# A convolution, SoLU and layer-norm kernel: separate scales for the first chunk's two pieces, another order of its loads, and the gain moved into the mean's matrix

## The chip, the cores and the metric

The kernel runs on one core of a Trainium2 chip. The metric is the time of one execution on the device in microseconds (us), and lower is better. The engines are TensorE (PE, with its weight loads PEld), VectorE (DVE), ScalarE (ACT) and GpSimd (POOL); SyncE (SP) issues the transfers.

## The reference

```
w   = softmax over the 7 taps of weight (8 heads x 7 taps)
y   = causal 7-tap convolution of x (8 x 4160 x 192); 24 channels share a head's taps
h   = y.reshape(33280, 192) @ w_in                    # 192 x 1024
s   = h * softmax(h)                                  # per token, over 1024
ln  = (s - mean(s)) / sqrt(var(s) + 1e-6) * g_ln
out = ln @ w_out                                      # 1024 x 192
```

All inputs and the output are float32.

## The kernel before

**Precision.** Each float32 matrix is split into two float16 parts, an upper and a lower one, and a product is three passes (upper by upper, upper by lower, lower by upper). A power of two scales each matrix first: x of a chunk by `s`, w_in by `t_in`, w_out by `t_out`. A scale comes from a sum of squares: an activation with an accumulator, a matmul with `ones` that adds over partitions (`total`, L95), one reduction, and four operations of one column on DVE (`root_power`, L105 to L112). `cv` holds five numbers of a chunk that follow from `s` and `t_in`, the exponent's factor among them. The inputs' words are taken apart by integer operations (class `Words`: exponents L447, mantissas L452, signs L480, join L489, value L496, powers L486, low words L458).

**Tiles.** The 33280 tokens are 260 tiles of 128. A tile goes through: twelve matmuls into its pair of PSUM banks `ph` (L736, L759; L749 for tiles 0 and 1), max over 1024 columns (DVE L790), exponential with its sum (ACT L797), product with its sum (DVE L807), cast to float16 (ACT L815), sum of squares (ACT L819), lower part (POOL L827), a transposing transfer to `pT` (L829), the matmuls of the second product `po` (L843), and its evacuation to SBUF (DVE L850), where two partial sums of 192 columns are added. Rows are finished by a group (L898, L902, L917, L921) and stored. I write max(3) for L790 of tile 3, mul(3) for its L807.

**Order.** Each engine's program is the order in which the code is written. Tiles 0 to 7, chunk 0 of x (1024 tokens, in two pieces of five windows of 112), have start-up code of their own: `first_two`, `second_two`, `third_two` and `fourth_two`. Then a loop takes three tiles a step, and `last_three` ends it. There are three pairs of PSUM banks (0 to 2) and two single banks. `emit_first` fills pairs for tiles 0 and 1, `emit_two` for the next two, and `hold` puts two groups of chunk 1's convolution (L281) into a pair. A pair is free again when its tile's mul has read it.

**Start-up.** SP issues the loads: x's first piece, w_in in two halves (512 KB each, `raw_in`), its last 64 rows (two of 256 KB), x's second piece (480 KB) between them, and w_out (`raw_out`, 1536 KB). DVE takes apart w_in's words, makes chunk 0's `s` and then `t_in`, writes the lower parts of the convolved x (L322; upper ones L313 on ACT) and of w_in (L647). POOL forms `cv` (L208) and w_out's values (`whole` L474, `value` L496, behind a `gate` that waits for the signs). `out_mean` (L701) multiplies w_out by `even`, whose every entry is 1/1024, so that each column's mean is in every partition; `out_upper` (L710) subtracts it. Before this, `out_powers` (L685) multiplies w_out's powers by g_ln.

Of the kernel before, what the change touches and what calls it, by code (L numbers as in the profile page):

```python
# [8 lines left out]
F16 = mybir.dt.float16  # L9
# [10 lines left out]
def kernel(  # L20
# [9 lines left out]
    nc = tc.nc  # L30
# [92 lines left out]
    class Chunk:  # L123
# [14 lines left out]

        def load(self, j):
# [52 lines left out]
        def scale_steps(self):  # L192
# [3 lines left out]
            ch = self.ch  # L196
            one = lambda nm, tag: sp.tile([P, 1], F32, name=f"{nm}_{ch}", tag=tag, bufs=2)
            self.all, self.s = one("xm", "xm"), one("s", "s")
            self.cv = cv = sp.tile([P, 5], F32, name=f"cv_{ch}", tag="cv", bufs=4)
# [3 lines left out]
                lambda: dve.tensor_reduce(self.all, self.tp, AX.X, ALU.add),  # L203
                *root_power(self.s, self.all, 2.0**30, 1e-14),
                lambda: dve.tensor_scalar(cv[:, 2:3], self.s, t_in, None, ALU.mult),
# [13 lines left out]
        def add_up(self, bank=None):  # L219
            self.tp = total(self.part[:, 0 : 2 * self.np], f"x{self.ch}", bank)  # L220
# [65 lines left out]
        def scale(self):  # L286
            return self.s[0:CW] if self.exact else 1.0 / TAPS
# [21 lines left out]
        def upper(self, pc, h, n, a, b):  # L309

            col, cuts = h * HD, self.cut(h * HD, n * HD)
            for e, z in zip(cuts, cuts[1:]):
                act.activation(  # L313
                    self.at(0, col + e, col + z, a, b), pc[:, :, e:z], AF.Copy,
                    scale=self.scale(),
                )

        def lower(self, pc, h, n, a, b):

            col, cuts = h * HD, self.cut(h * HD, n * HD)  # L320
            for e, z in zip(cuts, cuts[1:]):
                dve.scalar_tensor_tensor(  # L322
                    self.at(1, col + e, col + z, a, b), pc[:, :, e:z], self.scale(),
# [56 lines left out]
    nc.sync.dma_start(wb, weight.partition_broadcast(TJ))  # L380
    for j in range(NH):
        chunks[0].load(j)
# [4 lines left out]
    for j in range(2):  # L387
# [31 lines left out]
    even = cp.tile([P, P], F32, name="even")  # L419
    pool.memset(even, 1.0 / F)  # L420
# [6 lines left out]
    class Words:  # L427
# [37 lines left out]
        def squares(self, c, to):  # L465
# [4 lines left out]
                junk, self.e[:, c].bitcast(F32), AF.Square, scale=2.0**20, accum_out=to  # L470
# [65 lines left out]
    wi.powers(halves[0])  # L536

# [28 lines left out]
    words(halves[1])  # L566
    for h in c0.halves(1):
        c0.sum_squares(*h)
        if h[2] == 0:
            wi.powers(halves[1])  # L570
# [16 lines left out]
    chain0 = c0.scale_steps()  # L587
# [7 lines left out]
    def settle(a, z, got):  # L595
        for pc, hg in got:
            c0.lower(pc, *hg)
        for blk in (0, 2, 1):
            c0.turn(blk, a, z)

    pq = pair(1, "pq")
    going = convolve(*spans0[0], [pq[:, 0:512], pq[:, 512:F]])
    got0 = [next(going)]
    c0.add_up()
    got0 += going
    wi.squares(A, isq[:, 0:1])
    wi.signs(halves[0], wi.m)
    wi.exponents(Z)
    wi.powers(Z)
    for f in chain0[1:-3]:  # L610
        f()
    wi.squares(Z, isq[:, 1:2])
    for pc, hg in got0:
        c0.upper(pc, *hg)
    wi.value(halves[0], wi.m, dve)
    valued(halves[1])
    c0.open(0, None)
# [3 lines left out]
    tp = total(isq, "wi")  # L621
# [58 lines left out]
    def out_powers():  # L680


        woe = wo.e.bitcast(F32).rearrange("p (c d) -> p c d", d=D)
        for j in range(NFC):
            act.activation(  # L685
                woe[:, j], woe[:, j], AF.Copy, scale=gl[:, j : j + 1]
            )
# [8 lines left out]
    def out_mean():  # L696
# [841 lines left out]
```

## Time and profile before

| | |
|---|---|
| median of 3 runs | 1173.06 us (1172.7 to 1176.23) |
| profiled execution | 1174.77 us, of which the span is 1173.1 us |
| PE busy | 1135.2 us (97%) |
| DVE busy | 1019.3 us (87%) |
| ACT busy | 998.8 us (85%) |
| POOL busy | 877.6 us (75%) |
| granted PE clock | 1.00 |

The profiled execution is one of its own; the span is what its trace covers, and the 1.67 us between the two lie before the first and after the last record. Busy shares are over the whole span; the start-up code is the first 60 us of it.

### The profile page before, as it was taken

The numbers are of one execution on the slowest core, as the hardware profiler recorded it, in microseconds if no ns is written. First come the engines' busy times: TensorE is split into PE (matmuls) and PEld (weight loads), VectorE is DVE, ScalarE is ACT, GpSimd is POOL, SyncE is SP. The second block draws the span as 40 slices with busy tenths as digits, with TensorE's granted clock in tenths as the row PEclk, the third lists the DMA queues.
The fourth block names the chain that finished last, engine by engine and source line by source line (L and its number), as shares of the span: only waits on it lengthen the run. The fifth ranks groups of instructions, "written<-read, shape, count | busy, mean of one in ns | idle before, by whom it ended". The sixth has DMA issues, their size and how long they took to land.

```text
span 1173.1 us, 22240 instructions
## 1 busy us (share of the span) xinstructions
PE 1135.2 (97%) x7678; PEld 687.5 (59%) x7678; DVE 1019.3 (87%) x2057; ACT 998.8 (85%) x1773; POOL 877.6 (75%) x683
## 2 busy tenths in 40 slices
PE   5899999999999999999999999999999999999997
PEld 4455555555565665656556665665666566566555
DVE  8888798888989898898889989888898998788787
ACT  7998888887888888888888888888888889888885
POOL 1746788887878588787867888588788858855664
PEclk9999999999999999999999999999999999999999
DMA  7999999999999999999999999999999999999987
GB/s 220 180 185 174 181 206 204 206 185 201 197 206 205 184 191 193 222 182 200 206 196 192 195 215 202 186 204 204 209 196 193 202 193 173 178 165 194 181 161 175
DMA packets 727295, 226.95 MB, mean 193 GB/s; under 512 B 651518, under 2 KB 725774, under 8 KB 727182
## 3 DMA queue, kind: packets, MB, share of 16 engines
q1 hardware_dynamic: 727182, 225.53, 100.0%
q8 instruction: 60, 0.98, 0.3%
q14 instruction: 53, 0.43, 0.1%
HBM read 33.00 MB, written 25.56 MB: 50 GB/s over the span
## 4 chain that ended last, share of the span: by engine, by line
PE 70%; POOL 8%; DVE 6%; DMA 5%; issue 5%; ACT 4%; SPq 2%; POOLq 0%; DVEq 0%; ACTq 0%
PE po L843 32%; PE ph L736 29%; POOL p L827 5%; PE pc L281 5%; PE ph L759 4%; DMA pT<-p 4%; DVE ph L790 2%; DVE e L807 1%; ACT p L815 1%; ACT e L797 1%; ACT sq L819 1%; POOL xs L243 1%; DMA raw_in<-in_moe_w_in_dram 1%; POOL xr L240 1%; SPq L829 1%
## 5 line engine op out<-in xcount | busy, mean ns | idle before, releaser
L827 POOL TENSOR_TENSOR p<-e,p 128x1024 f16<-128x1024 f32 x259 | 552.8, 2138 | 237.6 <-ACT p L815 237.6
L843 PE MATMUL po<-ohl,pT 128*128 128x384 f16 (+1 forms) x4200 | 540.9, 285 | 15.3 <-DMA pT<-p 10.8
L843 PEld LDWEIGHTS <-pT 128*128 128x128 f16 x4200 | 379.3, 98 | 180.5 <-DMA pT<-p 15.5
L736 PE MATMUL ph<-whi,yT 128*128 128x512 f16 x1548 | 419.1, 380 | 5.5 <-DVE e L807 4.7
L790 DVE TENSOR_SCALAR_CACHE_REDUCE ph<-ph,cv 128x1024 f32<-128x1024 f32 x248 | 319.1, 1288 | 80.0 <-PE ph L759 63.0
L797 ACT ACTIVATE e<-ph,sm 128x1024 f32<-128x1024 f32 x260 | 289.5, 1113 | 103.8 <-DVE ph L790 96.1
L807 DVE SCALAR_TENSOR_TENSOR e<-ph,cv,e 128x1024 f32<-128x1024 f32 x248 | 317.0, 1278 | 22.2 <-ACT e L797 21.9
L736 PEld LDWEIGHTS <-yT 128*128 128x128 f16 x2064 | 192.4, 98 | 234.7 <-issue 35.6
L815 ACT CAST p<-e 128x1024 f16<-128x1024 f32 x260 | 269.9, 1038 | 31.7 <-DVE e L807 31.1
L819 ACT ACTIVATE sq<-e 128x1024 f32<-128x1024 f32 x260 | 273.5, 1052 | 0.1
L850 DVE TENSOR_REDUCE raw<-po 128x192 f32<-128x384 f32 x255 | 140.5, 551 | 16.9 <-PE po L843 16.6
L736 PE MATMUL ph<-wlo,yT 128*128 128x512 f16 x516 | 153.5, 379 | 0.0
L243 POOL TENSOR_TENSOR xs<-xr,xs 128x960 f16<-128x960 f32 (+1 forms) x56 | 107.6, 1922 | 1.4
L313 ACT ACTIVATE y<-pc 112x432 f16<-112x432 f32 (+5 forms) x140 | 62.9, 470 | 20.3 <-PE pc L281 11.7
L281 PE MATMUL pc<-xs,taps_hi 128*112 128x240 f16 (+1 forms) x448 | 73.0, 261 | 1.5 <-DVE xm L203 1.5
L759 PE MATMUL ph<-wlo,yT 64*128 64x512 f16 x269 | 74.0, 380 | 0.0
L322 DVE SCALAR_TENSOR_TENSOR y<-pc,y 112x432 f16<-112x432 f32 (+5 forms) x140 | 72.1, 532 | 0.7 <-ACT y L313 0.7
L181 DVE TENSOR_REDUCE xa<-xr 128x1 f32<-128x384 f32 x112 | 66.6, 617 | 3.5 <-DMA xr<-in_x_dram 3.5
L759 PE MATMUL ph<-wlo,y 64*128 64x512 f16 x251 | 68.6, 380 | 0.0
L281 PEld LDWEIGHTS <-taps_hi 128*112 128x112 f16 x448 | 52.4, 130 | 18.2 <-DVE xm L203 1.8
L240 POOL TENSOR_SCALAR xr<-xr,s 128x960 f32<-128x960 f32 (+1 forms) x56 | 57.6, 1029 | 3.0
L281 PE MATMUL pc<-xs,taps_lo 128*112 128x240 f16 (+1 forms) x224 | 58.5, 261 | 0.0
(145 smaller groups left out, 779.1 us busy)
## 6 DMA issues: line engine op xcount, KB each, us to landing
out_dram<-raw SPq DMA_DIRECT2D x127, 192.0 KB, 3.0
xr<-in_x_dram SPq DMA_DIRECT2D x41, 480.0 KB, 5.2
xr<-in_x_dram SPq DMA_DIRECT2D x22, 384.0 KB, 4.2
pT<-p SPq DMA_TRANSPOSE x260, 4.7
y<-yT SPq DMA_DIRECT2D x15, 140.0 KB, 3.1
y<-yT SPq DMA_DIRECT2D x15, 126.0 KB, 2.9
yT<-y SPq DMA_TRANSPOSE x102, 3.7
raw_out<-in_moe_w_out_dram SPq DMA_DIRECT2D x1, 1536.0 KB
```

The lines of the kernel that those rows point to most:

```text
L243: (2.1 * size + 0.2, lambda: pool.tensor_tensor(xl, r, h, ALU.subtract)),
L281: nc.tensor.matmul(o, tp[:, h + j, :], r, start=q == 0, stop=q == len(ops) - 1)
L736: nc.tensor.matmul(bank, lhs, w[:, r, n * 512 : (n + 1) * 512], start=start and j == 0, stop=stop and j == len(ops) - 1,)
L759: nc.tensor.matmul(banks_of(t)[n], y[q, t.off : t.off + P], wlo[q, 1, n * 512 : (n + 1) * 512], start=start, stop=not start,)
L790: dve.tensor_scalar(t.ph, t.ph, t.cv[:, 0:1], None, ALU.mult, ALU.min, accum_out=t.bias)
L797: act.activation(t.e, t.ph, AF.Exp, bias=t.bias, scale=-1.0, accum_out=grp.z[:, g : g + 1])
L807: dve.scalar_tensor_tensor(t.e, t.ph, t.cv[:, 3:4], t.e, ALU.mult, ALU.mult, accum_out=t.grp.s1[:, t.g : t.g + 1],)
L815: act.copy(t.p16[:, :, 0, :], t.halves)
L819: act.activation(junk, t.e, AF.Square, accum_out=t.grp.s2[:, t.g : t.g + 1])
L827: eng.tensor_tensor(t.p16[:, :, 1, :], t.halves, t.p16[:, :, 0, :], ALU.subtract)
L843: nc.tensor.matmul(t.po[:, 0:n], t.pT[:, a, :], w, start=j == 0, stop=j == len(ops) - 1)
L850: dve.tensor_reduce(t.grp.raw[:, t.g, :], t.po[:, 0 : 2 * D].rearrange("p (a d) -> p d a", a=2), AX.X, ALU.add,)
```

## The change

Seven edits, all in the start-up code except one that changes the numbering of pairs:

- w_in's four loads are issued ahead of x's second piece, and g_ln's load (`gl`) right behind w_out's.
- Chunk 0's two pieces have scales of their own. The first's chain follows the first piece's sums, the second's (`second_scale`) stands in `first_two`; a mixed `cvx` serves tile 4, which holds windows of both.
- w_out's low words are turned to numbers on POOL (`lows`) instead of ACT.
- `out_powers` goes. POOL writes g_ln/1024 into `even` (eight matrices), and `out_upper` multiplies by g_ln as it subtracts, in eight instructions in place of two. The squares of w_out take the largest g_ln as their factor.
- `emit_two` uses pairs 2 and 0, `hold` pair 1, and `hold` moves behind `emit_two`; the loop's pairs are renumbered in the same sense.
- Tiles 0 to 7 take the narrow pattern of `emit_out`, 24 matmuls of 192 columns into one sum instead of 16 of 384 or 192, and DVE copies it out instead of adding two sums.
- Some instructions of the start-up code change places (the second piece's squares and upper parts later, w_in's last mantissas earlier).

```diff
-    for j in range(NH):
-        chunks[0].load(j)
+    chunks[0].load(0)
+    for j in range(NH):
...
+    chunks[0].load(1)
     nc.sync.dma_start(
         raw_out.rearrange("p (c d) t -> p c (d t)", d=D),
...
+    nc.sync.dma_start(gl, g_ln.rearrange("(c p) -> p c", p=P))
...
+    pool.tensor_scalar(
+        even, gl.unsqueeze(2).broadcast_to([P, NFC, P]), 1.0 / F, 1.0,
+        ALU.mult, ALU.mult,
+    )
...
         def lows(self, c, scale):
-            act.activation(
-                self.low[:, c].bitcast(F32), self.low[:, c], AF.Copy, scale=scale
+            pool.tensor_scalar(
+                self.low[:, c].bitcast(F32), self.low[:, c], scale, 1.0,
+                ALU.mult, ALU.mult,
             )
...
+    def second_scale():
+        for f in c0.scale_steps(1)[1:]:
+            f()
+        cut = PW * CW
+        c0.mixed = cut // P
+        c0.cvx = sp.tile([P, 5], F32, name="cvx_0", tag="cvm", bufs=2)
+        pool.tensor_copy(c0.cvx, c0.cvs[1])
+        pool.tensor_copy(c0.cvx[0 : cut % P], c0.cvs[0][0 : cut % P])
+        for pc, hg in got0:
+            c0.upper(pc, *hg)
...
-    def out_powers():
-        woe = wo.e.bitcast(F32).rearrange("p (c d) -> p c d", d=D)
-        for j in range(NFC):
-            act.activation(
-                woe[:, j], woe[:, j], AF.Copy, scale=gl[:, j : j + 1]
-            )
+    def out_squares():
+        g = cp.tile([P, 1], F32, name="g_max")
+        dve.tensor_reduce(g, gl, AX.X, ALU.max, apply_absolute_value=True)
+        dve.tensor_scalar(g, g, 2.0**20, None, ALU.mult)
+        wo.squares(W, osq, g)
...
         for c in quarters:
-            dve.scalar_tensor_tensor(
-                wof[:, c], wof[:, c], 1.0,
-                mean[:, 0:D].unsqueeze(1).broadcast_to([P, NFC // 2, D]),
-                ALU.mult, ALU.subtract,
-            )
+            for j in range(c.start, c.stop):
+                dve.scalar_tensor_tensor(
+                    wof[:, j], wof[:, j], gl[:, j : j + 1], mean[:, 0:D],
+                    ALU.mult, ALU.subtract,
+                )
...
-        for slot, q in enumerate((t, u)):
+        for slot, q in ((2, t), (0, u)):
...
-            c.held = pair(2, f"pc_{c.ch}_{j}")
+            c.held = pair(1, f"pc_{c.ch}_{j}")
...
+        if not t.wide:
+            dve.tensor_copy(t.grp.raw[:, t.g, :], t.po[:, 0:D])
```

On SP, at the program's start, before (`xr_0` and `xr_1` are the two pieces of x):

```order
L160 DMA xr_0_77<-in_x_dram 128x4x192
L383 DMA raw_in<-in_moe_w_in_dram 128x1024
L160 DMA xr_1_82<-in_x_dram 128x5x192
L383 DMA raw_in<-in_moe_w_in_dram 128x1024
L388 DMA raw_in<-in_moe_w_in_dram 64x1024 x2
L392 DMA raw_out<-in_moe_w_out_dram 128x8x384
```

The same place now:

```order
L162 DMA xr_0_77<-in_x_dram 128x4x192
L403 DMA raw_in<-in_moe_w_in_dram 128x1024 x2
L408 DMA raw_in<-in_moe_w_in_dram 64x1024 x2
L162 DMA xr_1_85<-in_x_dram 128x5x192
L413 DMA raw_out<-in_moe_w_out_dram 128x8x384
L417 DMA gl<-in_moe_g_ln_dram 128x8x1
```

The second piece of x has moved behind w_in's last three loads, and `gl` stands behind `raw_out`.

On DVE in `first_two`, from max(0) to max(2), before (`ph_273`, `ph_274` and `ph_351` are tiles 0, 1 and 2):

```order
L790 TENSOR_SCALAR ph_273,sm_304<-ph_273,cv_166 128x1024
L489 SCALAR_TENSOR_TENSOR e_out<-raw_out,e_out 128x1536
L807 SCALAR_TENSOR_TENSOR e_306,s_0_269<-ph_273,cv_166,e_306 128x1024
L790 TENSOR_SCALAR ph_274,sm_320<-ph_274,cv_166 128x1024
L322 SCALAR_TENSOR_TENSOR y_0_0_190<-pr_201,s_165,y_0_0_190 112x5x96
...
L807 SCALAR_TENSOR_TENSOR e_322,s_0_269<-ph_274,cv_166,e_322 128x1024
L150 MEMSET xr_0_338 16x192
L790 TENSOR_SCALAR ph_351,sm_375<-ph_351,cv_166 128x1024
```

The same place now (`ph_270`, `ph_271`; L832, L849 and L342 are the lines of L790, L807 and L322):

```order
L832 TENSOR_SCALAR ph_270,sm_293<-ph_270,cv_0_138 128x1024
L518 SCALAR_TENSOR_TENSOR e_out<-raw_out,e_out 128x1536
L727 TENSOR_REDUCE g_max<-gl 128x1
L728 TENSOR_SCALAR g_max<-g_max 128x1
L832 TENSOR_SCALAR ph_271,sm_305<-ph_271,cv_0_138 128x1024
L849 SCALAR_TENSOR_TENSOR e_295,s_0_266<-ph_270,cv_0_138,e_295 128x1024
L207 TENSOR_REDUCE xm_1_312<-pr_201 128x1
...
L209 TENSOR_SCALAR cv_1_314<-s_1_313,t_in 128x1
L117 TENSOR_SCALAR cv_1_314<-cv_1_314 128x1
L342 SCALAR_TENSOR_TENSOR y_0_0_192<-pr_200,s_1_313,y_0_0_192 112x5x96
```

Nine instructions of one column are new (two of `g_max`, seven of the second scale), and max(1) stands ahead of mul(0).

On PE behind tile 1's matmuls, before (`pc_0_295` is the held convolution, `ph_351` tile 2):

```order
L759 MATMUL ph_274<-wlo,yT_197 128x512
L281 MATMUL pc_0_295<-xr_0_224,taps 112x5x24 x8
L736 LDWEIGHTS yT_197
L736 MATMUL ph_351<-whi,yT_197 128x512
...
L95 MATMUL pt_wo<-osq,ones 128x1
L701 MATMUL mean<-f_out,even 128x192 x8
```

The held convolution now stands behind tile 3 (`ph_365`):

```order
L801 MATMUL ph_271<-wlo,yT_191 128x512
...
L801 MATMUL ph_365<-wlo,yT_191 128x512
L294 MATMUL pc_0_376<-xr_0_222,taps 112x5x24 x8
L95 MATMUL pt_wo<-osq,ones 128x1
L743 MATMUL mean<-f_out,even 128x192 x8
```

It has moved from ahead of tiles 2 and 3 to a place between them and the mean, and it writes the pair that tile 1 leaves.

## Rows read from the trace of the kernel before

**Rows 1.** Windows: length, PE, PEld, DVE, ACT, POOL busy (instructions), clock, DMA share, GB/s.
```profile
0.00:50.00 50.00, 34.14 (x178) 21.14 (x179) 41.91 (x83) 41.29 (x75) 21.73 (x22) 1.00 0.91 216
640.00:1140.00 500.00, 499.45 (x3383) 300.08 (x3380) 434.82 (x860) 432.75 (x762) 383.58 (x290) 1.00 1.01 191
```

**Rows 2.** Waits of PE from 110 to 1140 us: total, times, longest.
```profile
PE po L843 <- DMA pT<-p: 7.6, 8, 1.9
```

**Rows 3.** Transfers that SP issued at 2.12, 2.66 and 3.14 us: size, time to landing.
```profile
raw_in<-in_moe_w_in_dram SPq DMA_DIRECT2D x1, 512.0 KB, 4.8
xr<-in_x_dram SPq DMA_DIRECT2D x1, 480.0 KB, 5.9
raw_in<-in_moe_w_in_dram SPq DMA_DIRECT2D x1, 512.0 KB, 8.1
```

**Rows 4.** Timeline of DVE: start, duration, instruction, idle time before it.
```profile
11.27 0.43 DVE L447 TENSOR_SCALAR e_in<-raw_in 128x512 int32<-128x512 int32 x1 [1.92 <-DMA raw_in<-in_moe_w_in_dram]
...
13.62 0.43 DVE L447 TENSOR_SCALAR e_in<-raw_in 128x512 int32<-128x512 int32 x1 [0.26 <-DMA raw_in<-in_moe_w_in_dram]
...
26.34 1.29 DVE L790 TENSOR_SCALAR_CACHE_REDUCE ph<-ph,cv 128x1024 f32<-128x1024 f32 x1
...
33.57 1.28 DVE L807 SCALAR_TENSOR_TENSOR e<-ph,cv,e 128x1024 f32<-128x1024 f32 x1 [0.27 <-ACT e L797]
...
34.99 1.20 DVE L790 TENSOR_SCALAR_CACHE_REDUCE ph<-ph,cv 128x1024 f32<-128x1024 f32 x1
...
37.40 1.29 DVE L790 TENSOR_SCALAR_CACHE_REDUCE ph<-ph,cv 128x1024 f32<-128x1024 f32 x1 [1.16 <-PE ph L759]
...
40.49 1.82 DVE L710 SCALAR_TENSOR_TENSOR f_out<-f_out,mean 128x768 f32<-128x768 f32 x2
...
45.74 1.28 DVE L790 TENSOR_SCALAR_CACHE_REDUCE ph<-ph,cv 128x1024 f32<-128x1024 f32 x1
...
50.37 0.16 DVE L203 TENSOR_REDUCE xm<-pc 128x1 f32<-128x4 f32 x1
...
51.64 1.27 DVE L807 SCALAR_TENSOR_TENSOR e<-ph,cv,e 128x1024 f32<-128x1024 f32 x1
```

**Rows 5.** Timeline of ACT in the start-up code.
```profile
20.38 1.34 ACT L313 ACTIVATE y<-pr,s 112x480 f16<-112x480 f32 x3
```

**Rows 6.** Timeline of PE in the start-up code.
```profile
10.63 1.94 PE L281 MATMUL pq<-xr,taps 128*112 128x120 f32 x8 [1.07 <-ACT taps L561]
...
26.72 1.89 PE L281 MATMUL pc<-xr,taps 128*112 128x120 f32 x16
30.78 0.60 PE L736 MATMUL ph<-whi,yT 128*128 128x512 f16 x2 [2.16 <-DVE e L807]
...
34.92 0.61 PE L736 MATMUL ph<-whi,yT 128*128 128x512 f16 x2 [1.71 <-DVE e L807]
...
37.53 2.85 PE L701 MATMUL mean<-f_out,even 128*128 128x192 f32 x16
```

**Rows 7.** Groups of instructions by shape: count, busy, mean ns, idle before.
```profile
L850 DVE TENSOR_REDUCE raw<-po 128x192 f32<-128x384 f32 x255 | 140.5, 551 | 16.9 <-PE po L843 16.6
L873 DVE TENSOR_SCALAR of<-po,t,o_inv 128x192 f32<-128x192 f32 x2 | 0.9, 470 | 0.0
L921 DVE TENSOR_SCALAR_CACHE_REDUCE raw<-raw,t 128x192 f32<-128x192 f32 x128 | 50.0, 404 | 0.0
L346 DVE COPY cvm<-cv 128x5 f32<-128x5 f32 x12 | 11.0, 920 | 0.0
L898 ACT ACTIVATE t<-z,cv 128x8 f32<-128x8 f32 x16 | 6.1, 380 | 0.0
L240 POOL TENSOR_SCALAR xr<-xr,s 128x960 f32<-128x960 f32 x42 | 44.9, 1069 | 2.9
L474 POOL TENSOR_TENSOR f_out<-m_out,raw_out 128x1536 f32<-128x1536 f32 x1 | 3.6, 3551 | 0.1
```

**Rows 8.** Timeline of POOL in the start-up code.
```profile
29.36 0.18 POOL L1141 COPY gate<-e_out 1x1 f32<-1x1 f32 x1 [2.46 <-DVE e_out L489]
```

More of the change, by code (lines that the diff above doesn't have):

```diff
@@ L190, in sum_squares, with scale_steps @@
             )
-        def scale_steps(self):
-            ch = self.ch
+        def scale_steps(self, piece=None):
+            ch = self.ch if piece is None else f"{self.ch}_{piece}"
             one = lambda nm, tag: sp.tile([P, 1], F32, name=f"{nm}_{ch}", tag=tag, bufs=2)
-            self.all, self.s = one("xm", "xm"), one("s", "s")
-            self.cv = cv = sp.tile([P, 5], F32, name=f"cv_{ch}", tag="cv", bufs=4)
+            m, s = one("xm", "xm"), one("s", "s")
+            cv = sp.tile([P, 5], F32, name=f"cv_{ch}", tag="cv", bufs=4)
+            self.ss.append(s)
+            self.cvs.append(cv)
             k = QS * (1e-6 * F) ** 0.5
@@ L536 @@
     wi.powers(halves[0])
+    wi.exponents(halves[1])
+    c0.add_up(a=0, z=2)
+    chain0 = c0.scale_steps(0)
+    for f in chain0[1:-3]:
+        f()
+    wi.signs(halves[0], wi.m)
+    wi.value(halves[0], wi.m, dve)
+    wi.exponents(Z)
+    wi.mantissas(halves[1])
+    wi.join(halves[1])
     taps = cp.tile([P, H, CW], F32, name="taps")
@@ L565 @@
         )
[L566 to L570, printed above, removed]
+    wi.powers(halves[1])
     def split_taps(q):
@@ L597, in settle @@
             c0.lower(pc, *hg)
-        for blk in (0, 2, 1):
+        for blk in (2, 1):
             c0.turn(blk, a, z)
     pq = pair(1, "pq")
[L602 to L605, printed above, removed]
+    got0 = list(convolve(*spans0[0], [pq[:, 0:512], pq[:, 512:F]]))
     wi.squares(A, isq[:, 0:1])
-    wi.signs(halves[0], wi.m)
-    wi.exponents(Z)
+    valued(halves[1])
+    wi.mantissas(Z)
     wi.powers(Z)
-    for f in chain0[1:-3]:
-        f()
[L612 to L617, printed above, removed]
+    wi.squares(Z, isq[:, 1:2])
+    c0.open(0, None)
+    ups = [f for pc, hg in got0 for f in c0.upper_steps(pc, *hg)]
+    for f in ups[:2]:
+        f()
+    c0.turn(0, *spans0[0])
+    for f in ups[2:]:
+        f()
     got1 = got0
     wo, W = Words(raw_out, "out"), slice(0, NFC * D)
-    tp = total(isq, "wi")
+    tp = total(isq, "wi", pair(2, "pt_wi")[:, 0:512])
     got0 = list(convolve(*spans0[1], [single("pr_0"), single("pr_1")]))
@@ L662 @@
         f()
+    wo.lows(W, 2.0**-32)
     wo.mantissas(W)
@@ L832, in emit_out @@
         t.po = single(f"po_{t.i}")
+        t.wide = t.grp.n > 1 and t.i >= PAIRED
         ops, per = [], NFC // NH
@@ L1106, in prepare @@
         t.cv = c.cvm if t.k == 0 else c.cv
+        if t.ch == 0 and t.k >= c.mixed:
+            t.cv = c.cvs[1] if t.k > c.mixed else c.cvx
         pos, n, t.g = t.slot
@@ L1142, in first_two @@
         wo.whole(W)
-        emit_mul(t)
-        out_powers()
+        out_squares()
         emit_max(u)
         emit_exp(u)
-        wo.squares(W, osq)
-        emit_hi(t)
+        numerators(t)
+        second_scale()
         settle_rest()
```

80 lines of the change are left out of this document (47 added, 33 removed).

## The prediction

> **What bounds the kernel now.** I first read the windows. From 640 to 1140 us PE is busy for 499.45 of 500 us, and in the first 50 for 34.14 only [rows 1]. In the steady loop PE is the bound, and its one wait of note is for the transposing transfer, 7.6 us in eight waits [rows 2]. No instruction of the loop changes except the numbers of its PSUM pairs. So the change acts on the start-up code, and it counts as far as it lets the loop begin earlier.
>
> Second, the timeline of DVE, since the start-up code is a race along one engine. DVE waits for w_in's second half at 11.27 us and for its last rows at 13.62 [rows 4], and then runs without a wait to max(0) at 26.34. So the first 26 us end when w_in has landed and DVE has worked through it. From there to max(4) at 45.74 the timelines of PE and DVE have to be read together: PE waits 2.16 us for mul(0) before tile 2 and 1.71 us for mul(1) before tile 3 [rows 6], and DVE in turn waits 1.16 us for tile 3's matmuls [rows 4]. Behind max(4) the chain is mixed, and PE fills up.
>
> **The change part by part.** I follow one clock, the time at which DVE starts a given max, and add what each edit does to it.
>
> *Loads.* The first half of w_in was issued at 2.12 us and landed 4.8 later, at 6.92; the second piece of x (480 KB) at 2.66 and 5.9 later, at 8.56; the second half of w_in at 3.14 and 8.1 later, at 11.24 [rows 3]. The three land in the order of issue, and x's piece takes 1.6 us of that row. With it behind w_in, the second half lands earlier by between nothing (if the loads share the engines evenly, whatever their order) and 2.7 us (the whole distance between the last two landings); I take 1.56. DVE's 0.26 us wait for the last rows [rows 4] goes as well, because the same two 256 KB loads follow at the same distance and DVE has five one-column operations of the first scale ahead of them. DVE has the same instructions between these words and max(0), in another order. **max(0): -1.82**, at about 24.5. The second piece of x now lands behind w_in, some 5 us later than 8.56; its convolution and its squares stand behind w_in's work, so this costs nothing while it lands before about 16 us.
>
> *The second scale.* Between max(0) and max(2) DVE gets the two operations of `g_max`: 0.3 us. It gets the seven operations of a scale chain; the same seven take from 50.37 to 51.64, that is 1.27 us [rows 4]. The lower parts of the second piece (L322) now need ACT's upper parts, which cannot start before the new `s`. `s` is there after five of the seven operations, 0.95 us, and a first upper part is half of 1.34 us [rows 5], 0.67, plus about 0.1 for the handover: 1.72 after the chain began, so DVE waits another 0.45. The 0.27 us that mul(1) waited for the exponential [rows 4] goes, as max(1) now stands ahead of mul(0). Together +0.30 + 1.27 + 0.45 - 0.27 = +1.75. **max(2): -0.07.** The gain of the loads is spent here.
>
> *The pairs.* Tile 2 takes pair 2, which is free, in place of one that waited for mul(0). Tile 3 waits for mul(0) where it waited for mul(1). mul(0) ended at 30.78, 4.44 after max(0); now max(1), 1.29, and `g_max`, 0.3, stand ahead of it: 24.5 + 4.44 + 1.59 = 30.5. Tile 3's matmuls then take as long as those of tile 2 before (34.92 - 1.71 - 30.78 = 2.43 us, rows 6), so they end near 32.9, ahead of max(2). DVE's wait of 1.16 us ahead of max(3) [rows 4] goes. **max(3): -1.23**, near 36.2.
>
> *The mean.* The held convolution, 1.89 us [rows 6], now waits for mul(1), which ended at 34.92 and ends 0.07 earlier, and the mean stands behind it: 34.85 + 1.89 + 2.85 [rows 6] = 39.6, and one small matmul between them. DVE would come to `out_upper` 3.09 us after max(3) (40.49 - 37.40, rows 4), near 39.3, and waits 0.4. The eight instructions of `out_upper` lie between 1.82 us in all, as now by columns [rows 4], and 8 x 0.40 = 3.2, if each costs what an operation on 192 columns with an accumulator does [rows 7]. I take 0.24 each, 1.92 in all, near the lower bound, since the inputs are those of L710 and nothing is accumulated: +0.1. **max(4): -0.73.**
>
> [...]
>
> *POOL and ACT.* The low words leave ACT and come to POOL, which the trace of before does not show. They cost between 1.07 x 1536/960 = 1.71 us [rows 7] and 3.55 (`whole`, rows 7); I take 1.7. They stand behind `cv` and ahead of the gate, where POOL waited for the signs for 2.46 us [rows 8]; that is their cover, so they cost nothing at 1.7 and up to 1.1 us at 3.55, or 1.7 and 3.55 without it. The end of POOL's work on w_out is awaited by the mean, which now also waits behind the held convolution. `even` costs POOL some 1.1 to 2.4 us by the same two rows, while POOL has nothing else before 25 us, if `gl` lands by about 21. `out_powers` stood on ACT ahead of the second exponential and the squares; its going is in the wait that mul(1) loses, and what is left of it meets the wait for the upper parts.
>
> *Evacuation.* Eight copies replace eight sums of 0.551 us. The nearest rows for 192 columns read from PSUM are L873's 0.470, and 0.404 for L921 from SBUF [rows 7]; so -0.08 to -0.15 each, 0 to -1.2 us in all if none or all of them bound. DVE is not always what ends there; I take -0.3. The narrow pattern has as many columns as the wide one, and eight more instructions per tile; I count +0.1.
>
> *Rows of chunk 0.* One operation of 0.38 us [rows 7] on ACT becomes three, for columns under different scales: +0 to +0.76 in the stretch from tile 6 to tile 10, where DVE and PE wait for ACT at times; I take +0.4.
>
> **Sum.** -0.73 - 0.3 + 0.1 + 0.4 = -0.53. From the profiled execution's 1174.77 that makes 1174.2. That execution is 1.71 above the median of the runs, so I give **1172.5 us** against 1173.06. A difference of 0.3% (3.5 us) is what a measurement can tell from no change.
>
> **The rivals.**
>
> *The copies wait for POOL (slower).* The one DVE copy in the loop, L346 with five columns, takes 0.920 us in the mean [rows 7], although an operation with one column out takes 0.16 [rows 4]: it waits for something, and POOL is busy beside it. If the eight copies of tiles 0 to 7 wait as long as this (0.75 us each over the 0.16), the start-up is 8 x 0.75 = 6.0 us longer: **1178.5**. It decides from 0.45 us per copy on. Against it: L346 reads SBUF, the copies read PSUM, and L873, also from PSUM, keeps to 0.470. [...]
>
> [...]
>
> *The gain reaches the end (faster).* If the second scale and its wait are hidden in full, the 1.75 us stay; and if the new phase of the loop loses half of the 7.6 us that PE waits for transfers [rows 2], another 3.8 go. With 2.0 of these: 1172.5 - 1.75 - 2.0 = **1168.7**. For it: such waits hang on small shifts of order. Against it: they can as well grow.
>
> *The loads change nothing.* w_in's half lands at 11.24 as before, if the queues take all loads at once. Then +1.56: **1174.1**, within the noise.
>
> **Chances and range.** The forecast gets 0.54, the loads without effect 0.16, the copies 0.07, the clock 0.07, the gain at the end 0.16. Faster by over 0.3% is the last, less or more: 0.16; slower 0.14; within 0.70. The range from 1168.5 to 1177 takes in the faster rival and the bounds of landing, `out_upper` and copies (-1.1, +1.3, -0.9), and leaves the copies' rival and the outer tails out.
>
> **What would show it.** DVE's L475 for w_in's second half should start near 9.7, max(0) near 24.5, max(2) near 34.9, max(3) near 36.2 with no wait, `out_upper` after a wait of some 0.4 us, max(4) near 45.0. The copies should take 0.4 to 0.5. The prediction is wrong if a max from tile 4 on stands over 2 us from its old time, if the copies take over 0.9, or if PE's waits for transfers in the loop differ by over 3 us from 7.6.

## The result, and the profile after

The changed kernel takes 1179.38 us in the median, and the kernel before, run beside it, 1174.41: ratio 1.004, with an interval of 1.0025 to 1.0055. It is 5 us slower, and the forecast was 1172.5 in a range to 1177. One execution of the changed kernel among 14, at 1690 us with a mean granted clock of 0.656, is left out of the ratio.

The profiled execution after took 1180.21 us, with a span of 1177.8. The windows, in the columns of [rows 1]:

```profile
0.00:50.00 50.00, 31.45 (x174) 19.20 (x175) 44.23 (x97) 36.06 (x63) 25.57 (x28) 0.97 0.82 204
640.00:1140.00 500.00, 497.94 (x3374) 299.51 (x3371) 434.58 (x860) 432.04 (x763) 382.36 (x291) 1.00 1.01 191
```

In the first 50 us VectorE is busy 2.3 us longer and PE 2.7 us less, and the granted clock is no longer 1.00. In the loop's window PE is busy for 1.5 us less. The timeline of DVE, line for line beside [rows 4]:

```profile
9.57 0.43 DVE L475 TENSOR_SCALAR e_in<-raw_in 128x512 int32<-128x512 int32 x1 [0.52 <-DMA raw_in<-in_moe_w_in_dram]
...
18.23 1.42 DVE L518 SCALAR_TENSOR_TENSOR m_in<-raw_in,e_in 128x512 int32<-128x512 int32 x1
...
25.22 1.29 DVE L832 TENSOR_SCALAR_CACHE_REDUCE ph<-ph,cv 128x1024 f32<-128x1024 f32 x1
...
26.42 2.66 DVE L518 SCALAR_TENSOR_TENSOR e_out<-raw_out,e_out 128x1536 int32<-128x1536 int32 x1
...
33.72 1.55 DVE L342 SCALAR_TENSOR_TENSOR y<-pr,s,y 112x480 f16<-112x480 f32 x3 [0.72 <-ACT y L327]
...
36.59 1.20 DVE L832 TENSOR_SCALAR_CACHE_REDUCE ph<-ph,cv 128x1024 f32<-128x1024 f32 x1
...
37.72 1.28 DVE L832 TENSOR_SCALAR_CACHE_REDUCE ph<-ph,cv 128x1024 f32<-128x1024 f32 x1
...
41.37 2.69 DVE L753 SCALAR_TENSOR_TENSOR f_out<-f_out,gl,mean 128x192 f32<-128x192 f32 x8 [0.54 <-PE mean L743]
...
47.29 1.28 DVE L832 TENSOR_SCALAR_CACHE_REDUCE ph<-ph,cvx 128x1024 f32<-128x1024 f32 x1
```

w_in's second half comes 1.70 us earlier (9.57 for 11.27). Two joins L518 are longer than any of their kind before: that of w_in's last rows takes 1.42 us, where the same 512 columns took 0.69, and that of w_out 2.66, where it took 1.75. In the kernel before they are L489:

```profile
20.08 0.69 DVE L489 SCALAR_TENSOR_TENSOR m_in<-raw_in,e_in 128x512 int32<-128x512 int32 x1
...
27.54 1.75 DVE L489 SCALAR_TENSOR_TENSOR e_out<-raw_out,e_out 128x1536 int32<-128x1536 int32 x1
```

The eight instructions of `out_upper` take 2.69 for 1.82. So max(0) is 1.12 us early, max(2) 1.60 late, max(3) 0.32 late and max(4) 1.55 late. The timeline of POOL shows what runs beside the two joins:

```profile
17.56 1.56 POOL L445 TENSOR_SCALAR even<-gl 128x1024 f32<-128x1024 f32 x1 [12.83 <-DMA gl<-in_moe_g_ln_dram]
...
25.73 1.76 POOL L486 TENSOR_SCALAR raw_out<-raw_out 128x1536 f32<-128x1536 uint32 x1
```

The first overlaps the join at 18.23, the second that at 26.42. When the joins begin, 0.89 us of the first and 1.07 us of the second are left, and the joins are longer by 0.73 and 0.91 us: by what is left of the POOL operation, less 0.16 each time. The timeline of PE, beside [rows 6]:

```profile
31.80 1.03 PE L778 MATMUL ph<-whi,yT 128*128 128x512 f16 x2 [3.61 <-DVE e L849]
...
36.57 1.86 PE L294 MATMUL pc<-xr,taps 128*112 128x120 f32 x16 [0.98 <-PE ph L801]
...
38.42 2.85 PE L743 MATMUL mean<-f_out,even 128*128 128x192 f32 x16
```

Behind a wait of 3.61 us two matmuls of 512 columns take 1.03 us, where they took 0.60: tile 3 runs at a lower clock (granted clock 0.79 from 32 to 38 us). Here this ends in time: from 38 to 44 us the granted clock is 1.00, and the convolution and the mean take 1.86 and 2.85 us, for 1.89 and 2.85. The copies and one of the three new operations of the rows, by shape:

```profile
L894 DVE COPY raw<-po 128x192 f32<-128x192 f32 x8 | 2.7, 348 | 0.0
```
```profile
71.52 0.38 ACT L944 ACTIVATE t<-z,cvx 128x1 f32<-128x1 f32 x1
```

### The profile page after: what moved, and what is told of

It reads as the page before. It is cut to its first block, busy times and chain, and to the rows that moved or that the text cites. A ratio compares the mean times of both kernels' runs of the same rounds, so it can differ in the third digit from the quotient of the medians.

```text
span 1177.8 us, 22381 instructions
## 1 busy us (share of the span) xinstructions
PE 1134.1 (96%) x7744; PEld 690.6 (59%) x7744; DVE 1021.0 (87%) x2072; ACT 995.7 (85%) x1766; POOL 880.4 (75%) x689
## 4 chain that ended last, share of the span: by engine, by line
PE 70%; POOL 7%; DVE 7%; DMA 7%; issue 4%; ACT 3%; SPq 2%; POOLq 0%; DVEq 0%; ACTq 0%
PE po L886 32%; PE ph L778 29%; DMA pT<-p 5%; PE pc L294 5%; PE ph L801 4%; POOL p L869 4%; DVE ph L832 2%; DVE e L849 1%; ACT p L857 1%; ACT e L839 1%; POOL xr L253 1%; POOL xs L256 1%; POOL t L957 1%; ACT sq L861 1%; DVE y L342 1%
## 5 line engine op out<-in xcount | busy, mean ns | idle before, releaser
L886 PE MATMUL po<-ohl,pT 128*128 128x192 f16 (+1 forms) x4264 | 540.9, 283 | 20.1 <-DMA pT<-p 15.1
L886 PEld LDWEIGHTS <-pT 128*128 128x128 f16 x4264 | 383.8, 98 | 181.5 <-DMA pT<-p 20.2
L832 DVE TENSOR_SCALAR_CACHE_REDUCE ph<-ph,cv 128x1024 f32<-128x1024 f32 x247 | 317.9, 1288 | 82.4 <-PE ph L801 65.7
L849 DVE SCALAR_TENSOR_TENSOR e<-ph,cv,e 128x1024 f32<-128x1024 f32 x247 | 315.8, 1278 | 20.9 <-ACT e L839 20.7
L896 DVE TENSOR_REDUCE raw<-po 128x192 f32<-128x384 f32 x247 | 136.3, 552 | 16.4 <-PE po L886 16.0
L342 DVE SCALAR_TENSOR_TENSOR y<-pc,y 112x432 f16<-112x432 f32 (+5 forms) x140 | 72.2, 532 | 0.7 <-ACT y L327 0.7
```

Of the source, the lines that this page charges most:

```text
L832: dve.tensor_scalar(t.ph, t.ph, t.cv[:, 0:1], None, ALU.mult, ALU.min, accum_out=t.bias)
L849: dve.scalar_tensor_tensor(t.e, t.ph, t.cv[:, 3:4], t.e, ALU.mult, ALU.mult, accum_out=t.grp.s1[:, t.g : t.g + 1],)
L886: nc.tensor.matmul(t.po[:, 0:n], t.pT[:, a, :], w, start=j == 0, stop=j == len(ops) - 1)
L896: dve.tensor_reduce(t.grp.raw[:, t.g, :], t.po[:, 0 : 2 * D].rearrange("p (a d) -> p d a", a=2), AX.X, ALU.add,)
```

## The experiments

Each was timed beside the kernel before (medians; before's own lay between 1173.6 and 1174.7). "Start" is the time at which max(10) begins in the run's profile, when the start-up code is over: 75.35 us in the first profile of before, 77.23 in that of the changed kernel.

### Who delays VectorE, and which part is worth what

**e1_even_act**: ScalarE writes g_ln/1024 into the mean's matrix, in its idle time at 19 us.

```diff
-    pool.tensor_scalar(
-        even, gl.unsqueeze(2).broadcast_to([P, NFC, P]), 1.0 / F, 1.0,
-        ALU.mult, ALU.mult,
-    )
...
     for h in c0.halves(1):
         c0.sum_squares(*h)
+    act.activation(
+        even, gl.unsqueeze(2).broadcast_to([P, NFC, P]), AF.Copy, scale=1.0 / F
+    )
```

> The changed kernel, with g_ln/1024 written into the mean's matrix by ScalarE (behind the second piece's squares, where it idles from 18.9 to 20.4 us) instead of GpSimd. Theory A (while a GpSimd operation reads SBUF, a VectorE operation with two SBUF inputs runs longer): the join L518 at 18.23 us takes 0.69 us instead of 1.42, max(0) starts at 24.5 instead of 25.22, every later max of the start-up code 0.7 earlier, and the time falls by about 0.7. Rival B (the join is long for another reason, since it also stands there for the first time): it stays at 1.4 and nothing moves. For the loop: theory C (its waits for transposing transfers hang on the phase alone) lets the waits of PE for pT between 110 and 1140 us lie anywhere from 5 to 12 us; rival D (the renumbered pairs make them) gives about 11 again.

The timeline of DVE in this run, the same two joins:

```profile
18.89 0.69 DVE L514 SCALAR_TENSOR_TENSOR m_in<-raw_in,e_in 128x512 int32<-128x512 int32 x1
...
26.36 2.60 DVE L514 SCALAR_TENSOR_TENSOR e_out<-raw_out,e_out 128x1536 int32<-128x1536 int32 x1
```

The first is back at 0.69, and the second, beside the low words, is not. w_in's half started 0.66 us later in this execution (10.23), and max(0) stood at 25.16: counted from there it is 0.72 earlier than in the changed kernel. Theory A holds, B falls. The median, 1178.71 (ratio 1.0038, 1.0023 to 1.0053), does not show a gain of 0.7, and with 1.8 us to either side it could not. In this profile the clock took more than the join gave:

```profile
36.45 3.43 PE L294 MATMUL pc<-xr,taps 128*112 128x120 f32 x16 [1.30 <-issue]
```

Here the low clock lay on the held convolution (granted clock 0.57 from 32 to 38 us), which took 3.43 us for 1.86, and max(4) came 3.00 late. PE's waits for pT were 5.8 us: D falls.

**e2_lows_act**: the low words on ScalarE again, behind the casts of the mantissas.

```diff
         def lows(self, c, scale):
-            pool.tensor_scalar(
-                self.low[:, c].bitcast(F32), self.low[:, c], scale, 1.0,
-                ALU.mult, ALU.mult,
+            act.activation(
+                self.low[:, c].bitcast(F32), self.low[:, c], AF.Copy, scale=scale
             )
...
-    wo.lows(W, 2.0**-32)
     wo.mantissas(W)
...
     wo.floats(W)
+    wo.lows(W, 2.0**-32)
```

> The changed kernel, with w_out's low words made into numbers by ScalarE again (behind the casts of w_out's mantissas) instead of GpSimd. Theory A: the signs of w_out, L518 at 26.42 us, take 1.75 us instead of 2.66, max(1) starts 0.9 earlier (28.3), max(2) near 35.7, and the time falls by 0.5 to 0.9. Rival B: L518 stays at 2.66. Waits for pT in the loop as in the first run: anywhere from 5 to 12 us (C), or 11 (D).

Two lines of DVE's timeline in this run:

```profile
26.81 1.76 DVE L517 SCALAR_TENSOR_TENSOR e_out<-raw_out,e_out 128x1536 int32<-128x1536 int32 x1
...
34.27 1.53 DVE L342 SCALAR_TENSOR_TENSOR y<-pr,s,y 112x480 f16<-112x480 f32 x3 [1.51 <-ACT y L327]
```

The join takes 1.76 us, as theory A says. But ScalarE is now later, and the lower parts wait 1.51 us for its upper parts instead of 0.72, so that max(2) is 2.14 late, or 1.75 when w_in's half, which started 0.39 later than in the changed kernel's profile, is allowed for; there it was 1.60. The 0.9 us are lost again by max(2). Median 1178.69, ratio 1.0044 (1.0027 to 1.006).

**e3_old_loads**: the changed kernel with before's order of the loads.

```diff
             w_in[0 : 2 * R, j * F : (j + 1) * F],
         )
+        if j == 0:
+            chunks[0].load(1)
...
-    chunks[0].load(1)
     nc.sync.dma_start(
         raw_out
```

> The changed kernel with the load order of before (second piece of x ahead of the second half of w_in). If the order of the loads is worth what it seems, the second half's exponents L475 start at 11.2 us instead of 9.57, max(0) starts 1.6 later (26.8), and max(4) 1.0 to 1.6 later (48.3 to 48.9); time +1.0 to +1.6 over the changed kernel. Rival: the start-up code has slack behind max(0), and max(4) moves by less than 0.5. Waits for pT in the loop: 5 to 12 us (C), or 11 (D).

The second half started at 10.88 us, max(0) at 25.79, max(4) at 47.81; the start was 78.93. The half is 1.31 later than in the changed kernel's profile, but max(0) only 0.57 and max(4) 0.52, hardly more than the rival allows, because the first join is short again (0.69 us at 19.53): POOL's operation ran from 17.59 to 18.65 and was over by then. It took 1.06 us there, and 1.22 to 1.75 in the ten other profiles that have it on POOL, where it meets DVE's operations with two inputs in SBUF. Median 1182.03, ratio 1.0065 (1.0052 to 1.0079), against 1.004 of the changed kernel and 1.0048 of its second timing (g2 below): some 2 to 3 us slower than with the new order, with an interval of about 2 to either side. By the times the new order is a gain; in the profiles it is worth half a microsecond at max(4).

**e4_wide**: the wide pattern and the summing evacuation for tiles 0 to 7.

```diff
-        t.wide = t.grp.n > 1 and t.i >= PAIRED
+        t.wide = t.grp.n > 1
```

> The changed kernel with the wide pattern and the summing evacuation for tiles 0 to 7, as before. If the narrow pattern gains what the trace shows (max(4) to max(8): 0.42 us), max(8) starts 0.3 to 0.5 later than in the changed kernel (67.7 to 67.8), and the time rises by 0.3 or not measurably. Rival: the narrow pattern's additional matmuls cost as much as the shorter copies save, and max(8) stays at 67.3. Waits for pT in the loop: 5 to 12 us (C), or 11 (D).

From max(4) to max(8) it takes 20.59 us (46.69 to 67.28), the changed kernel 20.05 (47.29 to 67.34): the narrow pattern gains 0.5. The median, 1177.38 (ratio 1.0031, 1.002 to 1.0042), points the other way, and is not told apart from 1.004. PE's waits for pT were 7.0, 10.0 and 5.8 us in e2, e3 and e4, anywhere in the range of theory C.

### The clock in the start-up

**c1_busy3**, **c2_busy2_lows** and **f1_pairs** repeat matmuls of the first tile of a pair in `emit_two`, to fill PE's waits. I overlooked that tiles 4 to 7 go through the same function.

```diff
             q.ph = pair(slot, f"ph_{q.i}")
+            for _ in range(2 if slot == 2 else 0):
+                emit_rows(q, True, True)
             emit_rows(q, True, False)
```

c1 has two repetitions; c2 has one, and the low words on ScalarE behind the second piece's squares; f1 is before with the pairs, `hold` behind `emit_two`, the narrow pattern and one repetition.

> The changed kernel, where TensorE computes the first eight matmuls of tile 2 twice more into the same banks before the real ones (16 more matmuls, 3.4 us, results overwritten), so that its wait of 3.6 us ahead of tile 3 is filled. Theory E (the idle wait drops TensorE's clock, and where the low clock falls on the held convolution it costs 1.45 us at max(4), as in the run with the matrix written by ScalarE): no stretch between 24 and 52 us at a granted clock below 1.00, tile 3's matmuls take 2.4 us, max(4) at 47.3 or less, and the median falls by about 1 to 1.5 us against the changed kernel (1177.5 to 1178.5 beside a before of 1174). Rival F: the low clock lies off the path in most executions; the median stays within 0.5 us of the changed kernel's.

> The changed kernel with one repetition of those eight matmuls (1.7 us) and with w_out's low words made by ScalarE in its idle 1.5 us at 18.9 us, so that GpSimd doesn't read SBUF beside w_out's signs. Theories A and E: L518 of w_out takes 1.75 us instead of 2.66, max(1) starts 0.9 earlier than in the changed kernel, max(4) near 46.4 (0.6 over before's 45.74) instead of 47.3, no low clock, and the median is 2 to 2.5 us below the changed kernel's, that is 2 to 3 above before. Rival: the low words delay ScalarE's next work (the low half of w_in at 20.4 us), and max(0) starts later by what is gained.

> The kernel before with three parts of the change: the pairs (tile 2 in pair 2, tile 3 in pair 0, the held convolution behind them in pair 1), the narrow pattern with copies in tiles 0 to 7, and one repetition of eight matmuls of tile 2 that keeps TensorE busy. By the parts' own figures: DVE's wait of 1.16 us ahead of max(3) goes, out_upper waits about 0.6 for the mean, and the copies give 0.4 by max(8): max(3) at 36.2, max(4) at 45.2, max(8) at 65.2, no low clock, time 1 us below before. Rival: the mean comes later than that (its convolution waits for mul(1)), max(4) at 45.7 or later, and the time equals before's.

All three missed: medians 1185.98 (1.0097, 1.0083 to 1.0111), 1182.56 (1.0066, 1.0054 to 1.0079) and 1178.83 (1.0037, 1.0025 to 1.0049). In tiles 4 and 6 PE has no idle time (in the changed kernel's first profile its one wait between 40 and 68 us is 1.79 us, ahead of tile 5), and the start rose to 84.1, 78.6 and 76.3 us. Up to max(4) they can still be read: in c2 the join of w_out is short and max(4) at 47.05, 1.3 late, not 0.6 (w_in's half started 0.65 later than in the changed kernel's profile). In f1 max(3) is at 36.17, max(4) at 45.24. In c1 the fill did not hold the clock: PE still waited 2.33 us ahead of the held convolution, and this took 3.37 us (granted clock 0.77 from 38 to 44 us). Behind the same 2.33 us in c2 it took 1.86.

**g1_filled**, **g3_pairs_filled** and **g4_filled_lows** mend this: only tiles 2 and 3 repeat. g1 is the changed kernel, g3 is f1 mended, g4 is the changed kernel with the low words placed as in c2. **g2_after_again** is the changed kernel itself.

```diff
             q.ph = pair(slot, f"ph_{q.i}")
+            for _ in range({2: 2, 3: 1}.get(q.i, 0)):
+                emit_rows(q, True, True)
             emit_rows(q, True, False)
```

(g3 and g4: one repetition for each of the two tiles.)

> The changed kernel, where TensorE computes the first eight matmuls of tile 2 twice more and those of tile 3 once more into their own banks before the real ones (24 more matmuls, 5.2 us, results overwritten; the runs before this repeated them in tiles 4 to 7 too, where TensorE has no idle time, and cost up to 7 us there). Its waits ahead of tile 3 (3.6 us) and ahead of the held convolution (1 to 2.3) shrink below 1 us. Theory E (these waits drop the clock, and on the convolution that costs 1.5 to 2 us): no stretch from 28 to 46 us below 1.00, convolution 1.9 us, max(4) at 47.3 or a little less, and the median 1 to 2 us below that of the changed kernel run beside it. Rival F: the clock matters little; the two medians lie within 0.7 us of each other.

> The changed kernel itself, beside the others on the same chip, with a second profile. By theory E the place of the low clock differs between executions: the span should come with max(4) between 1.5 and 4 us later than before's, and PE's waits for pT between 110 and 1140 us should differ from the first profile's 11.0 us. By rival D (the renumbered pairs make those waits) they are about 11 again. Median 1178 to 1180.

> The kernel before with the pairs, the held convolution behind tile 3, the narrow pattern and copies in tiles 0 to 7, and eight matmuls of tile 2 and of tile 3 repeated once, only there. max(3) 1.2 us earlier as in the run of these parts before this (37.40 to 36.17), out_upper after a wait of about 0.5, max(4) at 45.2, and now without the matmuls that tiles 4 to 7 had too much, max(8) at 65.2: 1 us below before in the profile's start-up, ratio 0.999. Rival: the loop gives it back, ratio 1.000 or more.

> The changed kernel with eight matmuls of tile 2 and tile 3 repeated once, only there, and w_out's low words on ScalarE in its idle time at 18.9 us. Theories A and E together: L518 of w_out 1.75 us, no low clock, max(4) 1.3 us later than before's, as in the run that also repeated matmuls in tiles 4 to 7, max(10) 1.6 later, and a median 1.5 to 2.5 above before, so 2.5 to 3.5 below the changed kernel. Rival F: the clock matters little and only the 0.9 us of L518 come back: 4 above before.

Medians beside a before of 1173.61: g1 1178.86 (1.0047, 1.003 to 1.0063), g2 1178.91 (1.0048, 1.0032 to 1.0063), g3 1174.92 (1.0015, 1.0001 to 1.0029), g4 1179.11 (1.0045, 1.0031 to 1.0058). In g1's profile the fill keeps the convolution at 1.87 us, but the median is that of the changed kernel. The clock, in the column before the last two, falls further on instead, on tile 5:

```profile
44.00:50.00 6.00, 5.28 (x26) 2.39 (x27) 5.23 (x10) 5.58 (x11) 2.63 (x1) 0.72 1.12 211
```

The mean clock of an execution is below 0.999 in 10 of g1's 12 timed ones and in 9 of g4's 12, as in 9 of g2's 10; averaged over the executions it is 0.997 in g1 and 0.995 in g2. So the fill took away only a part of the low clock. E's median missed and F's came true (g1 and g2 are 0.05 us apart), but since the clock was not held in g1, this does not decide between them; g4, 5.5 us above before, missed the 1.5 to 2.5 of A with E and the 4 of F. g2 came out as expected, with max(4) 2.89 late and 6.7 us of waits for pT. Its profile shows how bad the clock can be; its windows:

```profile
26.00:32.00 6.00, 2.39 (x9) 0.69 (x8) 5.79 (x13) 4.77 (x8) 4.25 (x3) 0.81 0.67 199
32.00:38.00 6.00, 5.79 (x19) 2.93 (x18) 5.25 (x11) 3.56 (x6) 5.75 (x8) 0.50 0.59 72
38.00:44.00 6.00, 6.00 (x34) 5.06 (x32) 3.55 (x12) 4.17 (x9) 4.25 (x3) 0.84 0.78 198
44.00:50.00 6.00, 4.21 (x12) 1.13 (x10) 5.93 (x13) 5.12 (x8) 3.14 (x2) 0.73 1.17 213
```

The convolution took 3.51 us, DVE waited 1.30 for `pt_wo` and 1.05 for the mean, and the start was 79.75. In g3 the start is 75.09, although its w_in landed 0.7 us later than before's: the pairs and the narrow pattern save 1 us there, and still the time is 0.15% above before's, as the rival had it. None of g3's 12 executions has a mean clock below 0.999. They take 1175.0 us in the mean, and the 20 executions of before beside them whose clock held as well take 1172.8. So at full clock g3 is 2.2 us slower, with a start that is 1 us earlier in its profile: neither the start-up nor the clock explains this loss. Its one profile does not show where it lies, and which part makes it (the renumbered pairs, the narrow pattern or the repeated matmuls) was not tried.

### Is the rest in the loop?

**h1 to h4** are further profiles, two of each kernel.

> The kernel before, a second profile. Theory C (waits for transfers vary between executions by themselves): PE's waits for pT between 110 and 1140 us between 4 and 9 us, the part behind max(259) up to 2 us longer or shorter than in the first profile, max(10) within 1 us of 75.35. Theory K (in the first profile before was an unusual execution): all three lie on one side.

> The kernel before, a third profile; as for the second: waits for pT 4 to 9 us, max(10) within 1 us of 75.35, no low clock between 30 and 60 us.

> The changed kernel, a third profile. Theory E: a stretch of low clock between 28 and 52 us again, max(10) 1.9 to 4.4 later than in before's profiles, the later the more of it lies on the held convolution. Theory C: waits for pT between 110 and 1140 us anywhere in 4 to 11 us; rival D: 9 or more.

> The changed kernel, a fourth profile; as for the third. If the loop and the tail are alike in both kernels (C), the mean of the four profiles from max(10) to the end equals that of before's three within 1 us; if the loop is slower by itself (D), it is 2 us or more longer.

All profiles of the two kernels, cut at max(10) and max(259) (us):

| | w_in's half | start | max(10) to max(259) | from max(259) on | PE's waits for pT |
|---|---|---|---|---|---|
| before | 11.27 | 75.35 | 1078.76 | 18.99 | 7.6 |
| h1, before | 10.06 | 77.63 | 1077.81 | 18.96 | 6.5 |
| h2, before | 10.62 | 77.77 | 1076.49 | 19.54 | 5.7 |
| changed | 9.57 | 77.23 | 1080.74 | 19.83 | 11.0 |
| g2, changed | 8.97 | 79.75 | 1078.83 | 19.82 | 6.7 |
| h3, changed | 9.81 | 78.70 | 1077.06 | 19.84 | 5.9 |
| h4, changed | 10.33 | 79.22 | 1076.00 | 19.78 | 6.1 |

In h3 and h4 the low clock came as expected (0.72 from 32 to 38 us and again from 44 to 50), and waits of 5.9 and 6.1 us speak against rival D. From max(10) to the end the changed kernel's four profiles are 1.1 us longer in the mean than before's three, between the 1 of C and the 2 of D. The expectation for h1 and h2 missed: before's clock falls too. h1's windows, PE and DVE:

```profile
32.00:38.00 6.00, 4.29 (x14) 1.29 (x12) 3.37 (x7) 6.00 (x10) 5.92 (x4) 0.75 0.73 126
38.00:44.00 6.00, 6.00 (x25) 5.22 (x25) 3.87 (x10) 3.05 (x8) 3.96 (x2) 0.68 1.09 262
```
```profile
38.09 4.70 PE L701 MATMUL mean<-f_out,even 128*128 128x192 f32 x16
```
```profile
42.91 1.82 DVE L710 SCALAR_TENSOR_TENSOR f_out<-f_out,mean 128x768 f32<-128x768 f32 x2 [2.01 <-PE mean L701]
```

The mean took 4.70 us for 2.85, DVE waited 2.01 for it, and from max(0) to max(10) it took 52.14 us for 49.01. The start came 2.28 later than in before's first profile although w_in landed 1.2 earlier. My prediction was worked out against an execution whose clock held, as it did in 49 of before's 83 timed ones. In the means of the table the changed kernel starts 1.8 us later (78.73 for 76.92), its loop is 0.5 longer (1078.16 for 1077.69; single executions differ by up to 4.7), and its last part 0.65. The landing varies as well: w_in's half starts between 10.06 and 11.98 us in the nine profiles of all kernels with the old order of the loads (11.04 in the mean), and between 8.97 and 10.33 in the eleven with the new order (9.77). So the new order gives 1.27 us in the mean, not the 1.70 of the first two profiles.

**c3_before_late**, **i1_before_early** and **i2_before_later** add nothing but operations of one column to the kernel before: ten ahead of max(4), ten ahead of max(0), 21 ahead of max(4).

```diff
     dve.tensor_scalar(o_inv, o_inv, float(F) ** 0.5, None, ALU.mult)
+    for _ in range(10):
+        dve.tensor_scalar(o_inv, o_inv, 1.0, None, ALU.mult)
```
```diff
         hold(c, 1)
+        for _ in range(10):
+            dve.tensor_scalar(o_inv, t_in, 1.0, None, ALU.mult)
         emit_max(t)
```

> The kernel before, with ten operations of one column (1.9 us, o_inv times 1) on VectorE ahead of max(4): the loop begins 1.9 us later, as in the changed kernel, and nothing else is changed. If a delay of the start is passed on one for one (G), the time is 1.9 us above before (ratio 1.0016), and the changed kernel's 5 us need another cause in the loop. If a later start alone changes the loop's waits for transfers by itself (H), the time is 4 to 5 above, or below before; PE's waits for pT then differ from 7.6 us by 3 or more in the profile.

> The kernel before with ten operations of one column (1.9 us) on VectorE directly ahead of max(0), before any tile is worked on. Everything behind waits for it alike, so that max(10) should come 1.9 us later (77.2 at full clock, beside 75.35), with the tiles in the same order of phase as before. Theory H (the loop runs longest or shortest by the phase in which it is entered, and before's phase is a short one): max(10) +1.9 and a median 1 to 2.5 above before, so that nothing is added in the loop. Theory L (any later start costs the loop two more, as with the ten operations ahead of max(4), whose mean time rose by 2.8 with 0.7 to 1.0 seen at max(10)): 3.5 to 4.5 above.

> The kernel before with 21 operations of one column (4 us) on VectorE ahead of max(4). Of the ten (1.9 us) at this place 0.7 to 1.0 were left at max(10) and 2.8 in the mean time. If what is left at max(10) grows one for one from there, it is 2.8 to 3.1 later; theory L: mean time 5 above before; theory H: anywhere from 2 to 6, not in step with max(10).

The starts were 76.03, 77.44 and 77.78, with the half of w_in at 10.92, 11.65 and 10.59; counted from equal landing that is 1.0, 1.7 and 3.1 later than before's first profile. The ratios are 1.0022 (1.001 to 1.0033), 1.0024 (1.0013 to 1.0036) and 1.004 (1.0027 to 1.0053), that is 2.6, 2.8 and 4.7 us, each with some 1.4 to either side. A later start is passed on in full, and by these medians each delay cost 1.1 to 1.6 us more than it shows at max(10). Each of these surpluses alone is about as large as its interval; that all three lie on one side speaks for L, and that they do not grow with the delay speaks against a loop that gets slower the later it begins; i1's 2.8 lies between the ranges of H and L. A part of the surplus goes with the clock, which is below 0.999 in 7 of 12, 10 of 12 and 7 of 9 executions. Where it held (5, 2 and 2 executions), these take 2.2, 2.7 and 4.3 us more than before's where it held, which leaves a surplus of 1.0 to 1.2. Another part is behind the loop: from max(259) on the three take 19.97 us in the mean, and before's three profiles 19.16.

## Why the prediction was wrong

**The loads** were right in kind: 1.70 us for 1.56 in the first profiles of the two kernels, where a part is luck, since the mean over all profiles is 1.27. By e3's times the order is a gain.

**"`even` costs POOL some 1.1 to 2.4 us ... while POOL has nothing else", and the low words "cost nothing at 1.7"**: this step failed first. I asked only whether POOL had the time. It had (1.56 and 1.76 us, as forecast), but beside these two operations a join on DVE, with two inputs in SBUF, takes 0.73 and 0.91 us longer, nearly what was left of the POOL operation when the join began; e1 and e2 give back each by itself, and in e3, where the first pair does not meet, the join takes 0.69 again. They stand on DVE, the engine that ends the start-up. max(0) is therefore at -1.12 and not at -1.82, and max(2) another 0.9 later. In the two profiles the joins go from 0.69 to 1.42 us and from 1.75 to 2.66, while mul(0), which reads PSUM too, began at 30.45 beside a POOL operation that ran from 29.42 to 32.96 and kept to 1.28. I had thought of POOL beside the copies alone.

**The second scale** was nearly right: the chain takes what it was said to, and the wait for the upper parts is 0.72 us for 0.45. The 0.1 in it for a handover from DVE to ACT was my estimate; behind `g_max` (its last operation ends at 29.33) ACT began 0.10 us later. From max(0) to max(2) the time grew by 2.72 (8.65 to 11.37), forecast 1.75; 0.91 of the miss is the join.

**The pairs** were right: DVE's wait ahead of max(3) is gone, -1.28 for -1.16.

**The mean**: its wait is right (0.54 for 0.4), the eight instructions are mis-sized. I took 0.24 us each, near the lower bound; they take 0.41 each and start 0.33 apart, 2.69 us in all, 0.87 more than the two of before. With a quarter of the columns one takes 0.41 us, where each of the two took 0.95; the 0.40 of L921, my upper bound, was the nearer row.

**Evacuation and rows** were mis-sized by a little: the copies take 0.348 us, -0.42 up to max(8) for -0.2 net. From max(8) to max(10), where the three operations of the rows stand, the time grew by 0.75 for 0.4; in g3, which has one operation as before, it grew by 0.2, so at most 0.55 of it is theirs.

**The sum to max(10)** was -0.53 and is +1.88 in the first profiles. The difference, 2.41, is 0.70 (first join) + 0.97 (second join, wait) + 0.73 (eight instructions, mean) - 0.12 (pairs) - 0.22 (evacuation) + 0.35 (rows).

**What comes behind max(10)** I put at nothing: the gain of the start was to be passed on, and no more. This step failed too. Of the 5 us only 1.9 are seen at max(10) in the first two profiles; the delays added to before lose 1.0 to 1.6 us more than shows there, and g3 loses 2.2 with an earlier start. The cause of this part stays open.

**Of the rivals**, the copies did not wait for POOL (0.348 us). The 0.07 for PE's clock was my estimate; in [rows 1] the granted clock reads 1.00. It did fall, in all four profiles of the changed kernel (0.79, 0.50, 0.72 and 0.72 from 32 to 38 us), and cost 0 to 3 us; what I had not seen is that it falls in two of three profiles of before as well (0.75 and 0.77 there). Over all timed executions the mean clock is below 0.999 in 41% of before's 83, which take 1175.1 us in the mean where the others take 1173.3, and in 21 of 23 of the changed kernel's; 1.8 us on half of the executions more is 0.9. One of my signs of being wrong came, PE's waits of 11.0 us for 7.6, but in the first profile alone: 5.9 to 6.7 in the three others.

**The account of the 5 us**: 1.9 from the start-up in the first two profiles, by parts and with each join tried alone (2.3 with the mean gain of the loads); about 0.9 that goes with more executions at a low clock, a correlation and not an experiment (g1's fill left the clock low in 10 of 12 executions); 0.3 more between the span and the time (2.0 for 1.72 in the mean of the runs). The remaining 1.5 to 2 are not settled. They fit the surplus of 1.0 to 1.6 that every delay of before showed, and the 0.65 us in the last tiles, where the last tile's matmuls waited for their transposing transfer and began 14.6 us after max(259) in all four profiles of the changed kernel, for 13.7 in two of before (in its third, h2, the clock fell there, to 0.80 from 1166 to 1172 us). Why the variants lose more than their start shows stays open. The profiles do not show before's loop itself as shorter: 1077.69 us in the mean, and 1078.05 in the three delays. The renumbered pairs are not needed for a surplus, since the delays have one without them, but g3's loss at full clock leaves open whether they or the narrow pattern add to it. No version beat before: g3, with the parts that gain at the start, is at 1.0015.

## What to carry to other kernels

Work that is moved to an engine with idle time is not free because that engine waits: here 1.56 and 1.76 us in POOL's idle time made two joins on DVE 0.73 and 0.91 us longer. Look at what runs beside it on the engine that ends the stage, and whether both read SBUF, as these did. An operation that is cut into eight has to be priced by a row of that small size (0.40 us for 192 columns; the eight took 0.41 each), not by its share of the columns (0.24). And a single profile of the kernel before is one draw: from max(0) to max(10) it took 49.01 us in one and 52.14 in another, so take two or three before a sum is made against one.

## What the runs showed of the hardware

The same two waits of PE, 2.16 and 1.71 us in one execution of before and 2.17 and 1.71 in another, ahead of the same matmuls, left the granted clock at 1.00 once, from 26 to 50 us, and were followed by a fall the other time (0.75 from 32 to 38 us and 0.68 from 38 to 44), at a price of 3.1 us from max(0) to max(10). And the joins on DVE, with two inputs in SBUF, that began while a POOL operation was reading SBUF took longer by about what was left of it: in the first profile 0.89 and 1.07 us of the POOL operations were left, and the joins took 0.73 and 0.91 us longer. In all 19 such pairs of the twelve profiles with this change, a join grew by what was left, less 0.13 to 0.17 us. So the price was here not the POOL operation's 1.56 or 1.76 us but what was left of it when the join came.
